# Turning the attention output in 32x32 word blocks on VectorE, with wo read by 8 KB rows

## The chip, the cores and the metric

The kernel runs on one core of a Trainium2 chip. The metric is the device time of one execution in microseconds. On one core there is no second die to compare with, so runs are compared through the kernel before, which ran on the same chip in the same rounds.

## The reference, cut to what matters

Decoding attention with grouped queries: 32 batches, 4 query rows each, 32 query heads on 4 key/value heads, 2048 cached keys, head size 128, all in bf16.

```python
q = (x @ wq).reshape(B, Sq, Hq, Dh)           # B=32, Sq=4, Hq=32, Dh=128
scores = einsum("bhqd,bhkd->bhqk", q, k) * Dh ** -0.5
p = softmax(scores)
o = einsum("bhqk,bhkd->bhqd", p, v)
return o.transpose(0, 2, 1, 3).reshape(B, Sq, Hq * Dh) @ wo
```

K and V are 134 MB, wq and wo 8.4 MB each. Every byte is read once.

## The kernel before: the parts that matter

All reads are issued by SyncE on one DMA queue. Each K or V load is 2 MB, 16 KB per partition. wo follows in 11 pieces after the last V, into buffers that K and V have left. Each piece of more than one head has 4 KB rows:

```python
WO = (4, 4, 4, 4, 4, 4, 2, 2, 2, 1, 1)             # heads per piece of wo
wo_v = wo.rearrange("(h p e) n -> p h (e n)", p=128, e=2)
...
    dst = wo_at(h0, m).rearrange("p (h n) -> p h n", n=2 * D)
    src = wo_v[:, h0 // 2:(h0 + m) // 2, :]        # D = 1024 bf16: rows of 4 KB
```

The output o of each batch comes out of P*V with (group, head, query) on partitions and the head size along the row. The out-projection needs the head size on partitions. Before, TensorE turns each batch with four matmuls against an identity, and ScalarE evicts the result:

```python
def o_evac(i):          # ScalarE: PSUM -> o_sb, scaled by 1/sum
    ...
def pe_ot(i):           # TensorE: four 128x64 matmuls per batch
    ...
            lhsT = o_sb.rearrange("p (d e) -> p e d", e=2)[:, e_, :]
            rhs = ident.rearrange("p (h u s) -> p u h s", u=2, s=Sq)[:, u, :, :]
    ...
def ot_evac(i):         # ScalarE: PSUM -> oT_sb
    ...
```

VectorE transposes every K tile (four 128x1024 word transposes a batch), takes the row maximum and turns the probabilities. TensorE also runs a few idle matmuls per batch.

## Time and profile before

Median 364.49 us of 3 runs (364.45 to 364.68).

| What | Reading before |
|---|---|
| Bytes read from HBM | 151.26 MB |
| DMA rate, 80 to 320 us | 428 GB/s, share 1.01 |
| DMA rate while wo arrives (slices 38 and 39) | 401 and 407 GB/s |
| VectorE busy, 80 to 200 us and 200 to 320 us | 92% and 87% |
| Last wait for wo ends | 358.66 us of a span of 362.4 us |

The DMA engines are full in every slice but the first and the last (90% or more by the page; their share is 1.01 from 10 to 355 us). No compute engine is: the busiest, TensorE, is busy for 85% of the span. The rate dips in slices 38 and 39, to 401 and 407 GB/s from 423 to 434, where wo with its shorter rows arrives.

The groups that the change removes, alters or adds to (the columns are line, engine, operation, tiles, shapes and count, then busy us and mean ns of one, then idle time before and its cause):

```profile
L373 POOL COPY PD_sb<-PT_sb 32x1024 f32<-32x1024 f32 x62 | 64.2, 1036 | 71.1 <-PE ps_r L384 46.3 <-DVE rinv L362 22.0
...
L406 ACT ACTIVATE oT_sb<-ps_r 128x128 bf16<-128x128 f32 x32 | 8.9, 278 | 106.6 <-PE ps_r L401 106.6
L401 PE MATMUL ps_r<-ident,o_sb 128*64 128x64 bf16 x128 | 8.1, 207 | 0.7 <-PEq L85 0.7
...
L362 DVE RECIPROCAL rinv<-ssum 128x1 f32<-128x1 f32 x32 | 3.9, 121 | 0.0
```

### The profile page before, as it was taken

Reading aid. Unit: us, or ns where it says so; the run is one execution under the profiler, and the core shown is the slowest. Engines: PE = TensorE matmul, PEld = TensorE weight load, DVE = VectorE, ACT = ScalarE, POOL = GpSimd, SP = SyncE. Lnnn points to the kernel's source line nnn. Section 1 sums busy time; section 2 is a strip of 40 time slices with the busy share of each in tenths; the row PEclk is TensorE's granted clock in tenths of the full one; section 3 lists DMA queues with packets and bytes.
Section 4 is the critical chain, followed back from the end, with each engine's and each line's share of the span. In section 5 each row is a group of like instructions: output and inputs, shape, how many; then the busy total and the mean of one; then the engine's idle time right before and its main releaser. Section 6 shows DMA issues by size and latency. Waiting matters only on the chain. (4 is left out here: it accounts for less than half of the span.)

```text
span 362.4 us, 6547 instructions
## 1 busy us (share of the span) xinstructions
PE 309.1 (85%) x2991; PEld 142.1 (39%) x2402; DVE 275.8 (76%) x275; ACT 111.4 (31%) x142; POOL 166.1 (46%) x261
## 2 busy tenths in 40 slices
PE   1987777899999999999999998888888889889896
PEld 1002000444444444444444444444333344449711
DVE  0028799999999999999999998898888888856200
ACT  1014222333333333333333333333322233334100
POOL 8002155255555555555555544445555555544000
PEclk9999999999999999999999999999999999999999
DMA  7999999999999999999999999999999999999995
GB/s 324 432 430 434 434 423 423 427 430 430 423 425 427 430 430 424 430 425 430 430 426 427 424 432 432 425 427 427 430 432 425 427 427 431 430 427 427 401 407 195
DMA packets 12589, 151.68 MB, mean 419 GB/s; under 512 B 1312, under 2 KB 1568, under 8 KB 3872
## 3 DMA queue, kind: packets, MB, share of 16 engines
q1 hardware_dynamic: 12432, 151.39, 98.7%
q10 hardware_dynamic: 144, 0.13, 0.1%
q8 instruction: 6, 0.10, 0.1%
q14 instruction: 7, 0.06, 0.0%
HBM read 151.26 MB, written 0.26 MB: 418 GB/s over the span
## 5 line engine op out<-in xcount | busy, mean ns | idle before, releaser
L324 DVE STREAM_TRANSPOSE KT_sb<-big 128x1024 f32<-128x1024 f32 x128 | 150.7, 1217 | 8.9 <-DMA big<-in_k_cache_dram 8.8
L351 ACT ACTIVATE P_sb<-ps_s,negmx 128x2048 bf16<-128x2048 f32 x32 | 82.2, 2568 | 85.3 <-DVE negmx L347 85.3
L16 PE MATMUL ps_s<-KT_sb,QD_sb 128*128 128x512 bf16 x384 | 103.7, 377 | 0.0
L373 POOL COPY PD_sb<-PT_sb 32x1024 f32<-32x1024 f32 x62 | 64.2, 1036 | 71.1 <-PE ps_r L384 46.3
L373 POOL COPY big<-PT_sb 32x1024 f32<-32x1024 f32 x61 | 63.7, 1045 | 59.6 <-PE ps_r L384 28.7
L346 DVE TENSOR_REDUCE mx<-ps_s 128x1 f32<-128x2048 f32 x32 | 73.3, 2292 | 11.0 <-PE ps_s L16 10.0
L384 PE MATMUL ps_r<-big 128*128 128x128 bf16 x1024 | 59.8, 219 | 8.7 <-PEq L85 8.6
L384 PE MATMUL ps_r<-big,PD_sb 128*128 128x128 bf16 x1024 | 59.8, 219 | 7.9 <-PEq L85 7.9
L384 PEld LDWEIGHTS ps_r<-big,PD_sb 128*128 128x128 bf16 x1024 | 58.0, 98 | 19.8 <-issue 18.7
L384 PEld LDWEIGHTS ps_r<-big 128*128 128x128 bf16 x1024 | 58.0, 98 | 19.7 <-issue 18.6
L337 PE MATMUL ps_s<-KT_sb,QD_sb 128*128 128x512 bf16 x128 | 48.3, 377 | 17.3 <-PEq L85 17.3
L337 PEld LDWEIGHTS ps_s<-KT_sb,QD_sb 128*128 128x128 bf16 x128 | 12.3, 96 | 103.1 <-issue 103.1
L361 DVE STREAM_TRANSPOSE PT_sb<-P_sb 128x1024 f32<-128x1024 f32 x32 | 39.9, 1246 | 15.1 <-ACT P_sb L351 15.1
L314 POOL COPY QD_sb<-QT_sb 32x64 f32<-32x64 f32 x128 | 29.6, 231 | 38.1 <-DVE QT_sb L293 20.7
L406 ACT ACTIVATE oT_sb<-ps_r 128x128 bf16<-128x128 f32 x32 | 8.9, 278 | 106.6 <-PE ps_r L401 106.6
L16 PE MATMUL ps_r<-QT_sb,ident 128*128 128x512 bf16 x132 | 33.7, 379 | 4.5 <-issue 4.4
L425 DVE CAST P_sb<-ps_s 128x512 bf16<-128x512 f32 x1 | 0.7, 690 | 22.1 <-PE ps_s L16 22.1
L401 PEld LDWEIGHTS ps_r<-ident,o_sb 128*64 128x64 bf16 x128 | 4.6, 109 | 31.2 <-issue 30.9
L275 DVE CAST KT_sb<-ps_r 128x512 bf16<-128x512 f32 x2 | 1.3, 686 | 20.0 <-PE ps_r L259 20.0
L391 ACT ACTIVATE o_sb<-ps_r,rinv 128x128 bf16<-128x128 f32 x32 | 11.7, 367 | 15.3 <-PE ps_r L384 13.4
L16 PE MATMUL ps_s<-big,oT_sb 128*128 128x512 bf16 x32 | 12.1, 379 | 0.7 <-ACT oT_sb L406 0.7
L416 PE MATMUL ps_s<-big,oT_sb 128*128 128x512 bf16 x30 | 11.4, 380 | 1.1 <-DMA big<-in_wo_dram 1.1
(41 smaller groups left out, 86.1 us busy)
## 6 DMA issues: line engine op xcount, KB each, us to landing
big<-in_k_cache_dram SPq DMA_DIRECT2D x32, 2048.0 KB, 16.9
big<-in_v_cache_dram SPq DMA_DIRECT2D x32, 2048.0 KB, 20.7
big<-in_wq_dram SPq DMA_DIRECT2D x4, 2048.0 KB, 13.9
big<-in_wo_dram SPq DMA_DIRECT2D x6, 1024.0 KB, 21.1
big<-in_wo_dram SPq DMA_DIRECT2D x3, 512.0 KB, 16.0
big<-in_wo_dram SPq DMA_DIRECT2D x2, 256.0 KB, 15.0
P_sb<-in_x_dram SPq DMA_DIRECT2D x1, 256.0 KB, 2.8
out_dram<-P_sb ACTq DMA_DIRECT2D x1, 128.0 KB, 1.8
```

The lines of the kernel that those rows point to most:

```text
L16: return eng.add_instruction(mybir.InstMatmult(name=nc.get_next_instruction_name(), engine=eng.engine, start_tensor_calc=start, stop_tenso ...
L314: p.op("pool", lambda e, s=src, d=dst: e.tensor_copy(d, s), waits if g == 0 else [], ("qd", i) if g == G - 1 else None)
L324: p.op("dve", lambda e, s=src, d=dst: e.transpose(d, s), waits, ("kt", i, c), gives="t_kt" if c == NCH - 1 else None)
L337: mm = lambda e, a_=(out_, lhsT, rhs), f=first, l=last: e.matmul(a_[0], lhsT=a_[1], rhs=a_[2], start=f, stop=l, skip_group_check=True)
L346: p.op("dve", lambda e: e.tensor_reduce(mx[:, i % 4:i % 4 + 1], ps_s[:, :], AX.X, ALU.max), [("qk", i)], ("mx", i))
L351: p.op("act", lambda e: e.activation(P_sb[:, :, :, :].rearrange("p t r w -> p t w r"), ps_s[:, :].rearrange("p (t w r) -> p t w r", w=2, r=R),
L361: p.op("dve", lambda e: e.transpose(dst, src), [("exp", i)] + ([("pd", i - 2, G - 1)] if i > 1 else []), ("pt", i))
L373: p.op("dve" if i >= B - 2 and g < i - B + 4 else "pool", lambda e, s=src, d=dst: e.tensor_copy(d, s), [("pt", i), free], ("pd", i, g))
L384: p.op("pe", lambda e: e.matmul(buf[:, 0:Dh], lhsT=pd_of(i)[:, t // 2, :, :, t % 2].rearrange("p g q -> p (g q)"), rhs=big[:, slot_of("v", ...
L391: p.op("act", lambda e: e.activation(o_sb[:, :], buf[:, 0:Dh], ACT.Copy, scale=rinv[:, i % 4:i % 4 + 1]), [("pv", i), ("rinv", i)] + ([("o ...
L406: p.op("act", lambda e: e.activation(oT_sb[:, :, :, i * Sq:(i + 1) * Sq].rearrange("p h e s -> p e h s"), buf[:, 0:128].rearrange("p (e h ...
L416: mm = lambda e, a=(out_, lhsT, rhs), h=h: e.matmul(a[0], lhsT=a[1], rhs=a[2], start=(h == 0), stop=(h == Hq - 1), skip_group_check=True)
```

## The change

The intent is to take the turning of o from TensorE and ScalarE. VectorE turns o in 32x32 blocks of 4-byte words (two bf16 each), four batches in one instruction (128x128 words), late in the kernel. For that, the rows of P*V are ordered by head mod 4, so that each block of 32 partitions holds one head mod 4. A partition of the turned o then belongs to four neighbouring rows of wo, so wo can be read by rows of 8 KB. The softmax sums still have the old row order, so TensorE permutes them with a one-column fp32 matmul before the reciprocal. The diff, cut to its core:

```diff
-        oT_sb = sbuf("oT_sb", [128, Hq // 2, 2, NT], BF16)
+        oT_sb = sbuf("oT_sb", [128, Hq // 4, 2, B, Sq, 2], BF16)
...
-        wo_v = wo.rearrange("(h p e) n -> p h (e n)", p=128, e=2)
+        wo_v = wo.rearrange("(h p e) n -> p h (e n)", p=128, e=4)
...
+            dst, src = wo_at(u0, m), wo_v[:, u0 // 4, u0 % 4 * D:(u0 % 4 + m) * D]
...
-            p.op("dve", lambda e: e.reciprocal(rinv[...], ssum[...]), [("exp", i)], ("rinv", i))
+        def pe_sum(i):
+            p.op("pe", lambda e: e.matmul(ring[i % 4][:, 511:512], lhsT=permf[:, :], rhs=ssum[:, i % 4:i % 4 + 1], ...))
+        def recip(i):
+            p.op("dve", lambda e: e.reciprocal(rinv[...], ring[i % 4][:, 511:512]), [("ss", i)], ("rinv", i))
...
-        def pe_ot(i): ...        # four matmuls per batch
-        def ot_evac(i): ...      # ScalarE eviction
+        def o_turn(b0, n):
+            for a in range(2):
+                src = words(QT_sb[:, b0:b0 + n, ...])...[:, :, a, :]
+                dst = words(oT_sb[:, :, a, b0:b0 + n, :, :]...)
+                p.op("dve", lambda e, s=src, d=dst: e.transpose(d, s), [("o", b0 + n - 1)], ...)
...
+            if 21 < i and 4 * (i - 22) + 4 <= i - LAG:
+                o_turn(4 * (i - 22), 4)
...
+        for b0, n in ((24, 4), (28, 2), (30, 1), (31, 1)):
+            o_turn(b0, n)
```

The copies that spread the probabilities now write runs of 8 words in place of 32, and the idle matmuls go from 4 of 512 columns to 5 of 384.

More of the change, by code (lines that the diff above doesn't have):

```diff
@@ L135, in bass_standalone__gqa_block_cached__sampling_kernel @@
     WO = (4, 4, 4, 4, 4, 4, 2, 2, 2, 1, 1)
+    IDLE = 384
     scale = float(Dh) ** -0.5
@@ L157, in bass_standalone__gqa_block_cached__sampling_kernel @@
         PT_sb = sbuf("PT_sb", [128, 2, T // 2, 32, 2], BF16)
-        PD_sb = sbuf("PD_sb", [128, T // 2, G, 32, 2], BF16)
-        o_sb = sbuf("o_sb", [128, Dh], BF16)
+        PD_sb = sbuf("PD_sb", [128, T // 2, 4, G, 8, 2], BF16)
         y_sb = P_flat[:, D:2 * D]
@@ L163, in bass_standalone__gqa_block_cached__sampling_kernel @@
         identf = sbuf("identf", [128, 128], F32)
+        permf = sbuf("permf", [128, 128], F32)
         mx = sbuf("mx", [128, 4], F32)
@@ L195, in slot_of @@
             return b % VS if kind == "v" else VS + b % KS
-        PF_sb = big[:, NS - 1, :, :].rearrange("p t d -> p (t d)").rearrange("p (t g q w) -> p t g q w", t=T // 2, g=G, q=32)
+        PF_sb = big[:, NS - 1, :, :].rearrange("p t d -> p (t d)").rearrange("p (t x g q w) -> p t x g q w", t=T // 2, x=4, g=G, q=8)
         for kind, b in loads:
@@ L208, in bass_standalone__gqa_block_cached__sampling_kernel, with wo_at @@
         wo_slot = [slot_of(kind, b) for kind, b in wo_for]
-        def wo_at(h, m):
-            return big[:, wo_slot[h // 8], :, :].rearrange("p t d -> p (t d)")[:, h % 8 * D:(h % 8 + m) * D]
-        wo_v = wo.rearrange("(h p e) n -> p h (e n)", p=128, e=2)
-        h0 = 0
+        def wo_at(u, m):
+            return big[:, wo_slot[u // 8], :, :].rearrange("p t d -> p (t d)")[:, u % 8 * D:(u % 8 + m) * D]
+        wo_v = wo.rearrange("(h p e) n -> p h (e n)", p=128, e=4)
+        u0 = 0
         for c, m in enumerate(WO):
-            assert h0 // 8 == (h0 + m - 1) // 8
-            kind, b = wo_for[h0 // 8]
-            if m > 1:
-                dst = wo_at(h0, m).rearrange("p (h n) -> p h n", n=2 * D)
-                src = wo_v[:, h0 // 2:(h0 + m) // 2, :]
-            else:
-                dst, src = wo_at(h0, 1), wo_v[:, h0 // 2, h0 % 2 * D:(h0 % 2 + 1) * D]
+            assert u0 // 4 == (u0 + m - 1) // 4
+            kind, b = wo_for[u0 // 8]
+            dst, src = wo_at(u0, m), wo_v[:, u0 // 4, u0 % 4 * D:(u0 % 4 + m) * D]
             p.dma("sp", lambda e, dst=dst, src=src: e.dma_start(dst, src),
                 [("kt", b, NCH - 1) if kind == "k" else ("pv", b)], ("wo", c), f"s_wo{c}")
-            h0 += m
-        assert h0 == Hq
+            u0 += m
+        assert u0 == Hq
         p.op("pool", lambda e: e.memset(ident[:], 0.0), [], "ident0")
@@ L233, in bass_standalone__gqa_block_cached__sampling_kernel @@
         p.op("pool", lambda e: e.tensor_copy(identf[:], ident[:]), ["ident"], "identf")
+        p.op("pool", lambda e: e.tensor_copy(
+            permf.rearrange("p (x g r) -> p x g r", x=4, g=G), ident.rearrange("p (g x r) -> p x g r", g=G, x=4)), ["ident"], "permf")
         p.op("pool", lambda e: e.memset(words(QD_sb[:, :, :, :, :, :].rearrange("p i a g q w -> p (i a g q w)")), 0.0), [], "qd0")
-        p.op("pool", lambda e: e.memset(words(PD_sb[:, :, :, :, :].rearrange("p t g q w -> p (t g q w)")), 0.0), [], "pd0")
-        p.op("pool", lambda e: e.memset(words(PF_sb.rearrange("p t g q w -> p (t g q w)")), 0.0), [], "pf0")
+        p.op("pool", lambda e: e.memset(words(PD_sb[:, :, :, :, :, :].rearrange("p t x g q w -> p (t x g q w)")), 0.0), [], "pd0")
+        p.op("pool", lambda e: e.memset(words(PF_sb.rearrange("p t x g q w -> p (t x g q w)")), 0.0), [], "pf0")
         for kt in range(KT):
@@ L270, in bass_standalone__gqa_block_cached__sampling_kernel @@
         for n, j in enumerate(QJ):
-            g, h = j // 2, j % 2 * 4
-            dst = q_sb[:, h:h + 4, :, g, :]
+            g, y = j // 2, j % 2
+            dst = q_sb.rearrange("p (x y) a g e -> p x y a g e", y=2)[:, :, y, :, g, :]
             src = ps_q(j).rearrange("p (h a e) -> p h a e", h=4, a=2)
@@ L354, in softmax_exp @@
                 [("negmx", i)] + ([("pt", i - 1)] if i else ["qproj"]), ("exp", i))
-            if i < L:
-                p.give("act", ("exp", i), "t_exp")
+            p.give("act", ("exp", i), "t_exp")
         def pt(i):
@@ L361, in pt @@
             p.op("dve", lambda e: e.transpose(dst, src), [("exp", i)] + ([("pd", i - 2, G - 1)] if i > 1 else []), ("pt", i))
-            p.op("dve", lambda e: e.reciprocal(rinv[:, i % 4:i % 4 + 1], ssum[:, i % 4:i % 4 + 1]), [("exp", i)], ("rinv", i))
+        def pe_sum(i):
+            p.op("pe", lambda e: e.matmul(ring[i % 4][:, 511:512], lhsT=permf[:, :], rhs=ssum[:, i % 4:i % 4 + 1], start=True, stop=True),
+                 ["permf"] if i == 0 else [], ("ss", i), [("t_exp", 1)] * (i == L))
+        def recip(i):
+            p.op("dve", lambda e: e.reciprocal(rinv[:, i % 4:i % 4 + 1], ring[i % 4][:, 511:512]), [("ss", i)], ("rinv", i))
         def pd_of(i):
@@ L370, in pd @@
                 rows = slice(32 * g, 32 * (g + 1))
-                src = words(PT_sb[rows, i % 2, :, :, :].rearrange("p t q w -> p t (q w)"))
-                dst = words(pd_of(i)[rows, :, g, :, :].rearrange("p t q w -> p t (q w)"))
+                src = words(PT_sb[rows, i % 2, :, :, :].rearrange("p t (x q) w -> p (t x) (q w)", x=4))
+                dst = words(pd_of(i)[rows, :, :, g, :, :].rearrange("p t x q w -> p (t x) (q w)"))
                 p.op("dve" if i >= B - 2 and g < i - B + 4 else "pool", lambda e, s=src, d=dst: e.tensor_copy(d, s), [("pt", i), free], ("pd", i, g))
@@ L384, in pe_pv @@
             p.op("pe", lambda e: e.matmul(
-                buf[:, 0:Dh], lhsT=pd_of(i)[:, t // 2, :, :, t % 2].rearrange("p g q -> p (g q)"),
+                buf[:, 0:Dh], lhsT=pd_of(i)[:, t // 2, :, :, :, t % 2].rearrange("p x g q -> p (x g q)"),
                 rhs=big[:, slot_of("v", i), t, :], start=(t == 0), stop=(t == T - 1)),
@@ L390, in o_evac, with oT_of @@
             buf = ring_of["o", i]
-            p.op("act", lambda e: e.activation(o_sb[:, :], buf[:, 0:Dh], ACT.Copy, scale=rinv[:, i % 4:i % 4 + 1]),
-                 [("pv", i), ("rinv", i)] + ([("oT", i - 1)] if i else []), ("o", i), gives="t_o")
-        def pe_ot(i):
-            buf = ring_of["ot", i] = slot()
-            for e_ in range(2):
-                for u in range(2):
-                    out_ = buf[64 * u:64 * (u + 1), 64 * e_:64 * (e_ + 1)]
-                    lhsT = o_sb.rearrange("p (d e) -> p e d", e=2)[:, e_, :]
-                    rhs = ident.rearrange("p (h u s) -> p u h s", u=2, s=Sq)[:, u, :, :]
-                    p.op("pe", lambda e, a=(out_, lhsT, rhs): e.matmul(a[0], lhsT=a[1], rhs=a[2], start=True, stop=True),
-                         [], ("oT", i) if e_ == u == 1 else None, [("t_o", 1)] if e_ == u == 0 else [])
-        def ot_evac(i):
-            buf = ring_of["ot", i]
-            p.op("act", lambda e: e.activation(
-                oT_sb[:, :, :, i * Sq:(i + 1) * Sq].rearrange("p h e s -> p e h s"),
-                buf[:, 0:128].rearrange("p (e h s) -> p e h s", e=2, s=Sq), ACT.Copy),
-                [("oT", i)], ("ot", i))
+            dst = QT_sb[:, i, :, :, :, :].rearrange("p a h s w -> p (a h s w)").rearrange("p (a d w) -> p a d w", a=2, w=2)
+            src = buf[:, 0:Dh].rearrange("p (d a w) -> p a d w", a=2, w=2)
+            p.op("act", lambda e: e.activation(dst, src, ACT.Copy, scale=rinv[:, i % 4:i % 4 + 1]), [("pv", i), ("rinv", i)], ("o", i))
+        def o_turn(b0, n):
+            for a in range(2):
+                src = words(QT_sb[:, b0:b0 + n, :, :, :, :].rearrange("p b a h s w -> p b (a h s w)")).rearrange(
+                    "p b (a d) -> p b a d", a=2)[:, :, a, :]
+                dst = words(oT_sb[:, :, a, b0:b0 + n, :, :].rearrange("p h b s w -> p h b (s w)")).rearrange("p h b s -> p b h s")
+                p.op("dve", lambda e, s=src, d=dst: e.transpose(d, s), [("o", b0 + n - 1)], ("ot", b0 + n - 1) if a else None)
+        def oT_of(u):
+            return oT_sb[:, u // 4, u % 4 // 2, :, :, u % 2].rearrange("p b s -> p (b s)")
         def oproj(c):
@@ L413, in oproj @@
                 for j in range(2):
-                    out_, lhsT, rhs = ps_s[:, NC * j:NC * (j + 1)], oT_sb[:, h // 2, h % 2, :], wo_at(h, 1)[:, NC * j:NC * (j + 1)]
+                    out_, lhsT, rhs = ps_s[:, NC * j:NC * (j + 1)], oT_of(h), wo_at(h, 1)[:, NC * j:NC * (j + 1)]
                     if j == 0:
@@ L436, in bass_standalone__gqa_block_cached__sampling_kernel @@
         starts = []
+        idle_rhs = ident[:, :].unsqueeze(1).to_broadcast([128, IDLE // 128, 128])
         for i in range(B + LAG):
@@ L445, in bass_standalone__gqa_block_cached__sampling_kernel @@
                 softmax_max(i)
-            if 0 < j < B - LAG:
-                pe_ot(j - 1)
-                ot_evac(j - 1)
+            if 0 < i < B:
+                pe_sum(i - 1)
             if i < B:
-                pe_idle(16 if i < LAG else 4, ring[len(used) % 4], q_flat, [("qb", 3, 1), ("qs", 3)] if i == 0 else [])
+                pe_idle(20 if i < LAG else 5, ring[j % 4][:, 0:IDLE], idle_rhs, [("qb", 3, 1), ("qs", 3)] if i == 0 else [])
                 softmax_exp(i)
+            if 0 < i < B:
+                recip(i - 1)
             if i < L:
                 kt(i + 1, (2, 3))
+            if 21 < i and 4 * (i - 22) + 4 <= i - LAG:
+                o_turn(4 * (i - 22), 4)
             if i < B:
@@ L458, in bass_standalone__gqa_block_cached__sampling_kernel @@
                     pe_pv(j, t)
-                if j >= B - LAG:
-                    pe_ot(j - 1)
-                    ot_evac(j - 1)
+                if i == B:
+                    pe_sum(L)
                 o_evac(j)
+            if i == B:
+                recip(L)
             if 0 < i <= B:
                 pd(i - 1)
-        pe_ot(L)
-        ot_evac(L)
+        for b0, n in ((24, 4), (28, 2), (30, 1), (31, 1)):
+            o_turn(b0, n)
         for c in range(len(WO)):
```

## The prediction

364.49 us measured, less 0.5 us for wo, gives the 364.0 us.

> **What bounds the kernel now.** DMA bandwidth, from about 3 us to 359 us. The page's 40 slices show the DMA engines at 0.99 or 1.0 in every slice but the first and last, moving 423 to 434 GB/s. The kernel must move 151.4 MB.[...] The DMA issue view shows K and V loads (2 MB each, about 4.9 us of transfer) landing 17 and 21 us after issue: three to four loads are always queued, so the queue doesn't run dry. VectorE is busy 93% of 80 to 200 us but only 86% of 220 to 320 us, because it has run ahead of the data. The chain that ended last finishes with wo: last piece landed about 358.7 us, then matmul, eviction (0.69 us) and the output DMA (1.8 us).
>
> **What the change does.**
> - Removed, 32 times each: four TensorE 128x64 matmuls (0.25 us a group), their ScalarE eviction (0.28 us). Idle matmuls go from 4x512 to 5x384 columns, about 0.06 us less by the 0.215 us spacing. None of these lies on the DMA path.
> - Added, 32 times: a one-column fp32 matmul (estimate 0.3 us, from 0.14 us weight load and 0.27 us for the trace's f32 128x128 matmul); the reciprocal now reads PSUM (0.12 us before, perhaps 0.15).
> - Added once: VectorE turns. 128x1024 words take 1.22 us, so 128x128 words should take about 0.2 us: 2.4 us in six iterations in which VectorE has about 1.4 us spare each, and about 1 us at the end.
> - PD/PF copies: runs of 8 words instead of 32 (GpSimd 1.04 us now). If they take 1.0 to 1.5 us, GpSimd goes from about 5.1 to at most 7 us of a 9.8 us period: off the path.
> - wo by 8 KB rows: the only part on the path. The packet records show 614 ns for 16 KB and 161 ns for 4 KB (median), so about 10 ns a packet and 151 ns per 4 KB: an 8 KB packet is estimated at 312 ns. Six pieces (6.3 MB) change from 1536 packets of 4 KB to 768 of 8 KB, over 16 engines: 15.5 us becomes 15.0 us. The last 2 MB keep 4 KB and 2 KB packets.
>
> **On the critical path:** -0.5 us from wo. Everything else falls in slack: the out-projection starts at 343.7 us, needs 64 x 0.215 = 13.8 us, and waits for wo from 350.6 us on; wo pieces wait about 15 us in the queue after issue, so a tail a few microseconds later on VectorE or TensorE costs nothing. Turning the last batches should let the out-projection start about 0.5 us earlier, which only lengthens its waits.
>
> **Predicted:** 364.0 us, range 363.2 to 365.0. Faster by over 2%: 0.01; within 2%: 0.97; slower by over 2%: 0.02.
>
> **What would show each step.** Slices 38 and 39, 401 and 407 GB/s now, rise to about 415 to 422; wo packets of 8 KB take about 312 ns; last wo landing near 358.2 us. DMA share stays 0.99 or more. ScalarE busy falls about 9 us, the four-matmul group and its eviction vanish; GpSimd copies stay below 1.5 us; VectorE turns near 0.2 us, the end still waiting for wo in the chain.
>
> **What would make it wrong.** GpSimd copies doubling or worse with short runs, delaying P*V, V buffers and so loads; the fp32 one-column matmul or its weights costing much more than 0.3 us and holding TensorE; turns with 32-byte strided writes taking several times 0.2 us, delaying the last K buffers and starving wo; 8 KB packets running no faster than 4 KB[...].

## More of the kernel before

The page's first part has the busy time of each engine; of the second part the DMA rows are shown (40 slices of the span, tenths of busy DMA engines, then GB/s); of the third part, the DMA queues with packets, MB and share:

```profile
PE 309.1 (85%) x2991; PEld 142.1 (39%) x2402; DVE 275.8 (76%) x275; ACT 111.4 (31%) x142; POOL 166.1 (46%) x261
...
DMA  7999999999999999999999999999999999999995
GB/s 324 432 430 434 434 423 423 427 430 430 423 425 427 430 430 424 430 425 430 430 426 427 424 432 432 425 427 427 430 432 425 427 427 431 430 427 427 401 407 195
...
q1 hardware_dynamic: 12432, 151.39, 98.7%
q10 hardware_dynamic: 144, 0.13, 0.1%
q8 instruction: 6, 0.10, 0.1%
q14 instruction: 7, 0.06, 0.0%
```

The end of the kernel, first in the chain of waits (start, duration, what), then in the timeline (last P*V and the last wait for wo):

```profile
341.77 15.61 DMA big<-in_wo_dram
357.38 0.04 issue
357.42 0.39 PE ps_s L416
```

```profile
338.38 3.73 PE L384 MATMUL ps_r<-big 128*128 128x128 bf16 x64
...
358.66 0.10 PEld L416 LDWEIGHTS ps_s<-big,oT_sb 128*128 128x128 bf16 x1 [0.48 <-DMA big<-in_wo_dram]
```

The out-projection has to wait for wo to land. From the wait that ends at 357.38 us, eight matmuls, the eviction and the output DMA remain.

## The result

364.56 us median of 6 runs (364.51 to 364.67), against 364.44 us of 6 runs of before (364.27 to 364.68). The ratio is 1.0003, with a 95% interval of 0.999 to 1.0016: the same time. A ratio here is the mean time of one kernel's runs over that of the other's of the same rounds, so it is not quite the ratio of the medians.

The page of the changed kernel, the same lines:

```profile
PE 308.9 (85%) x3002; PEld 147.4 (41%) x2338; DVE 279.1 (77%) x295; ACT 102.7 (28%) x110; POOL 165.9 (46%) x262
...
DMA  8999999999999999999999999999999999999994
GB/s 325 425 432 434 432 430 423 428 423 430 428 423 428 432 426 430 428 427 428 428 427 430 429 426 428 426 430 432 426 428 426 428 431 430 426 428 421 416 416 159
...
q1 hardware_dynamic: 11664, 151.39, 98.4%
q8 instruction: 6, 0.10, 0.1%
q10 hardware_dynamic: 144, 0.13, 0.1%
q14 instruction: 8, 0.07, 0.0%
```

Slices 38 and 39 rose from 401 and 407 to 416 and 416 GB/s, and q1 has 768 packets fewer: wo by longer rows works. Yet the last slice fell from 195 to 159 GB/s: less was moving at the very end. VectorE has 20 more instructions, and the second instruction queue carried 8 packets in place of 7.

The groups that took the place of the removed ones:

```profile
L377 POOL COPY PD_sb<-PT_sb 32x1024 f32<-32x1024 f32 x62 | 64.3, 1036 | 70.1 <-PE ps_r L388 45.2 <-DVE PT_sb L359 22.0
...
L362 PE MATMUL ps_r<-ssum,permf 128*128 128x1 f32 x64 | 8.9, 208 | 0.0
...
L366 DVE RECIPROCAL rinv<-ps_r 128x1 f32<-128x1 f32 x32 | 5.0, 158 | 0.2 <-PE ps_r L362 0.2
...
L404 DVE STREAM_TRANSPOSE oT_sb<-QT_sb 128x128 f32<-128x128 f32 x14 | 3.3, 274 | 0.0
```

The end in the chain of waits, then in the timeline:

```profile
332.70 25.12 DMA big<-in_wo_dram
357.82 0.05 issue
357.87 0.39 PE ps_s L414
```

```profile
339.29 3.73 PE L388 MATMUL ps_r<-big 128*128 128x128 bf16 x64 [1.19 <-PEq L85]
...
359.13 0.10 PEld L414 LDWEIGHTS ps_s<-big,oT_sb 128*128 128x128 bf16 x1 [0.51 <-DMA big<-in_wo_dram]
```

Both ends are about 0.45 us later than before (357.82 against 357.38, and 359.13 against 358.66). The surprise is the other line: P*V of the last batch begins 0.9 us later than before and TensorE idles 1.19 us ahead of it. It needs the last V load. So the delay was there before any of wo was used.

### What the packet records show

The trace also holds every DMA packet, with start, duration, size and queue, but not which of the 16 DMA engines moved it. (From here on, "engine" without a name is a DMA engine.) The records hold 1312 packets of 4 bytes for the 82 transfers of the page, 16 each. So we take it that every load is split over the 16 engines and that each ends its share with such a packet, its mark. By this reading, which fits the time between marks below (eight 16 KB packets of 614 ns are 4.91 us), the mean of these 16 marks tells when the average engine was done, and the end of the last data packet when the slowest was. (The groups of 16 are taken in order of time. An engine that is far behind can exchange a mark with the next load; for the ends, the last data packet is used.) In us of the span:

```
                                        before    after
last V load: mean of 16 engines         336.38   336.55
last V load: slowest engine             337.74   338.65
end of wo:   mean of 16 engines         357.45   357.25
end of wo:   slowest engine             358.16   358.64
slowest, from last V to end of wo        20.42    19.98
```

So the slowest engine needs 0.44 us less for wo, and the mean engine finishes 0.20 us earlier. But the slowest engine came to wo 0.91 us later. The records say when it fell back. In the load just ahead of the last V (mean mark at 331.60 us), the slowest engine went from 1.26 us behind the mean to 2.17 us behind. In that time the records hold an 8 KB packet of the second instruction queue, and right behind it a 16 KB data packet of twice the usual 614 ns:

```
start us   bytes   ns     queue
 332.18     8192    325   q14 (instructions)
 332.50    16384   1273   q1  (V data)
```

If both ran on one engine, the pair cost it 0.325 + 1.273 - 0.614 = 0.98 us, close to the 0.91 us by which the slowest engine fell back. From 50 us on, every 16 KB data packet above 900 ns, 10 in before and 12 after the change, starts within 15 ns of the end of an instruction packet. Before has no instruction packet between 302 and 335 us.

The packet times in the traces of before and after, so far as they matter here:

| Packets | ns each |
|---|---|
| data on q1, 16 KB, 8 KB, 4 KB and 2 KB (medians) | 614, 312, 161 and 84 |
| instructions on q8, 16 KB | 1018 to 1102 |
| instructions on q14, 8 KB, from 50 us on | 309 to 362 |
| 16 KB of data right behind an 8 KB instruction packet, from 50 us on | 960 to 1273 |

The marks support that one engine paid, and show which. Sorted by time, 15 of the 16 marks of that load come 4.89 to 4.90 us after those of the load before it, and the last one 5.86 us after: the engine that was already last lost 0.97 us. They also show why it was last. Before holds two pairs of the same form (a fetch of 325 ns, then a data packet of 1273 ns), at 80.62 and 206.46 us, when 61 and 187 of VectorE's recorded instructions had started. Each made a single mark later by 0.97 us: one went from 0.09 to 1.06 us after the fourth-earliest mark of its load, and later one from 1.09 to 2.06 us, which made it the last. In the changed kernel the three pairs come at VectorE's 62nd, 187th and 312th. So these look like VectorE's own fetches, all on one engine, which is the slowest because of them.

The ends follow the slowest engine. The waits end about 0.5 us after the last data packet (358.66 against 358.16, and 359.13 against 358.64).

### The profile page after: what moved, and what is told of

It is laid out like the page before. It is cut to its first block, busy times and chain, and to the rows that moved or that the text cites. A ratio compares the mean times of both kernels' runs of the same rounds, so it can differ in the third digit from the quotient of the medians.

```text
span 362.8 us, 6454 instructions
## 1 busy us (share of the span) xinstructions
PE 308.9 (85%) x3002; PEld 147.4 (41%) x2338; DVE 279.1 (77%) x295; ACT 102.7 (28%) x110; POOL 165.9 (46%) x262
## 2 busy tenths in 40 slices
DMA packets 11822, 151.69 MB, mean 418 GB/s; under 512 B 1312, under 2 KB 1568, under 8 KB 2336
## 5 line engine op out<-in xcount | busy, mean ns | idle before, releaser
L16 PE MATMUL ps_s<-KT_sb,QD_sb 128*128 128x512 bf16 x384 | 105.0, 381 | 0.0
L377 POOL COPY PD_sb<-PT_sb 32x1024 f32<-32x1024 f32 x62 | 64.3, 1036 | 70.1 <-PE ps_r L388 45.2
L377 POOL COPY big<-PT_sb 32x1024 f32<-32x1024 f32 x61 | 63.2, 1036 | 60.4 <-PE ps_r L388 35.9
L336 PE MATMUL ps_s<-KT_sb,QD_sb 128*128 128x512 bf16 x128 | 48.7, 381 | 21.9 <-PEq L85 21.9
L16 PE MATMUL ps_r<-ident 128*128 128x384 bf16 x173 | 33.3, 325 | 0.0
L362 PEld LDWEIGHTS ps_r<-ssum,permf 128*128 128x128 f32 x64 | 11.9, 187 | 24.8 <-issue 23.1
L397 ACT ACTIVATE QT_sb<-ps_r,rinv 128x128 bf16<-128x128 f32 x32 | 11.8, 368 | 24.1 <-PE ps_r L388 21.6
L414 PE MATMUL ps_s<-big,oT_sb 128*128 128x512 bf16 x32 | 12.2, 380 | 2.2 <-DMA big<-in_wo_dram 1.2
L16 PE MATMUL ps_s<-big,oT_sb 128*128 128x512 bf16 x32 | 12.1, 379 | 0.0
L247 PE MATMUL ps_r<-ident 128*128 128x384 bf16 x32 | 10.3, 323 | 0.0
```

The source lines that it names most:

```text
L16: return eng.add_instruction(mybir.InstMatmult(name=nc.get_next_instruction_name(), engine=eng.engine, start_tensor_calc=start, stop_tenso ...
L336: mm = lambda e, a_=(out_, lhsT, rhs), f=first, l=last: e.matmul(a_[0], lhsT=a_[1], rhs=a_[2], start=f, stop=l, skip_group_check=True)
L362: p.op("pe", lambda e: e.matmul(ring[i % 4][:, 511:512], lhsT=permf[:, :], rhs=ssum[:, i % 4:i % 4 + 1], start=True, stop=True), ["permf"] ...
L377: p.op("dve" if i >= B - 2 and g < i - B + 4 else "pool", lambda e, s=src, d=dst: e.tensor_copy(d, s), [("pt", i), free], ("pd", i, g))
L397: p.op("act", lambda e: e.activation(dst, src, ACT.Copy, scale=rinv[:, i % 4:i % 4 + 1]), [("pv", i), ("rinv", i)], ("o", i))
L414: mm = lambda e, a=(out_, lhsT, rhs), h=h: e.matmul(a[0], lhsT=a[1], rhs=a[2], start=(h == 0), stop=(h == Hq - 1), skip_group_check=True)
```

## The theories

- **Theory A.** The 20 turns made VectorE's instruction stream longer by enough to need one more 8 KB piece. Its fetch runs on a DMA engine that is already the slowest, and makes it 0.9 us later. All engines are full while wo arrives (share 1.00 from 335 to 355 us in the changed kernel), so, by this theory, the slowest doesn't make up for it, and its lateness reaches the end of the kernel. It eats the 0.44 us that the longer rows save.
- **Rival B.** The longer rows of wo save nothing at the end, or lengthening VectorE's stream costs nothing: something else ends last.
- **Rival C.** The turns cost VectorE's time, or its order, and that delays loads.
- **Rival D.** Small added instructions late in the kernel disturb the loads by themselves, on whatever engine.

In the expectations below, times of fetches were read with the packets' clock set 0.5 us later than here; "332.7 us" there is the fetch at 332.18 us. A "page" there stands for the 8192 bytes of one q14 packet; that the length of the stream, or reaching a "page boundary", brings the next one is the theory that the runs test.

## The experiments

Each was run in 5 rounds beside before.

### The changed kernel again

No edit.

> The changed kernel itself, as the base for the three runs beside it on the same chip. All theories: 364.4 to 364.7 us, ratio to before 1.000 to 1.001, an 8 KB instruction fetch at about 332.7 us of the span, the slowest of the 16 DMA engines finishing the last V load about 2.1 us after the mean engine, while the others' last is 1.3 us after it.

364.80 us median (364.49 to 364.93), before 364.42, ratio 1.0007. Fetch at 332.52 us, slowest engine 2.47 us behind at the last V. The numbers repeat, with the slowest engine a little further behind.

### Turns merged from 20 instructions to 4

```diff
-            for a in range(2):
-                src = ...[:, :, a, :]           # one half, 32 words per batch
+            src = words(QT_sb[:, b0:b0 + n, ...])            # both halves
+            dst = words(oT_sb[:, :, :, b0:b0 + n, :, :]...).rearrange("p h a b s -> p b a h s")
...
-            if 21 < i and 4 * (i - 22) + 4 <= i - LAG:
-                o_turn(4 * (i - 22), 4)
+            if i == 27:
+                o_turn(0, 24)
...
-        for b0, n in ((24, 4), (28, 2), (30, 1), (31, 1)):
+        for b0, n in ((24, 6), (30, 1), (31, 1)):
```

> The changed kernel with its 20 VectorE turns merged into 4, so that VectorE's stream is 16 instructions shorter; the same words are turned. Theory A (the turns lengthened VectorE's instruction stream past one more 8 KB page; its fetch at 332.7 us runs on the DMA engine that is already last and makes it 0.9 us later, which eats the 0.45 us that wo's longer rows save): the fetch disappears or moves to after the last wo packet, the slowest engine is back at about 1.3 us behind the mean, and the time falls by 0.6 to 0.9 us to 363.7 to 364.0 us, 0.5 us below before. Rival B (wo's longer rows save nothing at the end because something else ends last, TensorE or the final pieces): unchanged, 364.4 to 364.7. Rival C (the loss is VectorE's time for the turns): they still cost about 3 us in all, so at most 0.2 us better.

363.74 us median (363.58 to 363.82), before 364.42, ratio 0.9981 (0.9967 to 0.9994). That is 1.06 us less than the changed kernel. The result is correct. The queue line and the start of the last P*V of this run:

```profile
q14 instruction: 7, 0.06, 0.0%
```

```profile
338.48 3.73 PE L388 MATMUL ps_r<-big 128*128 128x128 bf16 x64 [0.50 <-PEq L85]
...
343.04 0.38 PE L412 MATMUL ps_s<-big,oT_sb 128*128 128x512 bf16 x1 [0.83 <-DVE oT_sb L402]
```

The fetch near 332 us is gone (one at 335.87 us stays, which the changed kernel has too, at 335.92), the last P*V starts within 0.1 us of where it did before (338.48 against 338.38), and the out-projection starts 0.9 us earlier than in before or after. The slowest engine is 1.33 us behind at the last V, as before. Rival B expected no change. Rival C, whose bound was 0.2 us, doesn't fit 1.06 us. But the turns take 2.8 us here and 4.2 us in the changed kernel, so this run alone doesn't exclude it; the runs with late memsets below do.

### wo by 4 KB runs in the changed kernel

Two pieces of wo that lie in one buffer exchange halves, so that each reads two runs of 4 KB per partition. DMAs, bytes and instructions stay the same in number.

```diff
+            if m == 4:
+                r = c % 2 * 2 * D
+                dst = big[:, wo_slot[u0 // 8], :, :]....rearrange("p (h n) -> p h n", h=2)[:, :, r:r + 2 * D]
+                src = wo_v[:, c // 2 * 2:c // 2 * 2 + 2, r:r + 2 * D]
...
+            if WO[c] == 4:
+                hs = [c // 2 * 8 + c % 2 * 2 + k for k in (0, 1, 4, 5)]
```

> The changed kernel with its first six wo pieces read as two 4 KB runs a partition in place of one 8 KB run; the same number of DMAs, bytes and instructions per piece. Theory A: wo's packets return from 312 to 161 ns for half the bytes, every engine needs 0.43 to 0.5 us more for wo, and the time rises to 364.9 to 365.1 us. Rival B: wo's rows don't show at the end, 364.4 to 364.7 us.

365.28 us median (364.99 to 365.37), ratio 1.0021 to before. It is 0.48 us over the changed kernel beside it. The absolute time missed the expected 364.9 to 365.1 because the base was 364.80, not 364.56. The packets are back at 161 ns for 4 KB, and the slowest engine takes 20.40 us for wo in place of 19.98.

### Both edits

> Both edits: 4 merged turns and 4 KB rows. Theory A: the two effects add, so about 0.45 us over the run with merged turns alone, 364.1 to 364.5 us, near before. Rival B: equal to the changed kernel. If the effects don't add (difference under 0.2 us), the theory of one slowest engine that sets the end is wrong.

364.29 us median (364.00 to 364.35), ratio 0.9994. The four runs form a square, medians in us:

| | with the extra fetch (20 turns) | without (4 turns) | difference |
|---|---|---|---|
| wo by 8 KB rows | 364.80 | 363.74 | 1.06 |
| wo by 4 KB runs | 365.28 | 364.29 | 0.99 |
| difference | 0.48 | 0.55 | |

The effects add. The rows are worth about 0.5 us on the critical path, as predicted, and whatever came with the 20 turns costs about 1.0 us.

### The kernel before with 20 VectorE memsets where the turns are

```diff
+            if 21 < i <= 27:
+                pad(2, "dve")       # memsets of one scratch column each
...
+        pad(8, "dve")               # ahead of the last turn of o
```

> The kernel before with 20 one-column VectorE memsets of a scratch tile, placed where the change puts its 20 turns (two in each of six late iterations, eight at the end). Nothing else changes. Theory A: VectorE's stream crosses the same page boundary, an 8 KB instruction fetch appears at about 332 us of the span, the slowest DMA engine falls about 0.9 us further behind, and the time rises by 0.6 to 0.95 us to 365.0 to 365.4 us. Rival B: VectorE has slack,[...] 364.3 to 364.6 us.

365.13 us median (365.01 to 365.52), before 364.36, ratio 1.0025 (1.0011 to 1.0039). The extra 8 KB fetch is there, but at 337.93 us, not near 332. It fell in the wo phase: the slowest engine was 1.40 us behind at the last V and 1.55 us behind at the end of wo, where before it is 0.72 us behind. The cost of 0.77 us is as expected; the time of the fetch was missed. Its pair is cheaper here: the fetch took 326 ns and the 4 KB packet of wo behind it 496 ns in place of 161, so 0.66 us in all where a 16 KB packet of V made it 0.98.

### The same memsets after VectorE's last copy

```diff
         oproj_out()
+        pad(20)
```

> The same 20 memsets, all placed after VectorE's last copy, when the last wo packet has landed. The stream is as long as in the run with pads in the loop. Theory A: the page boundary is reached only after the last data packet, so any fetch comes too late to delay a load; 364.3 to 364.7 us. If the program's length itself costs (for example at the start), 0.5 us or more slower.

365.07 us median (364.86 to 365.43), ratio 1.002. This expectation failed, and it is the most telling run. The queue line and VectorE's timeline at the end:

```profile
q14 instruction: 8, 0.07, 0.0%
```

```profile
360.28 0.69 DVE L433 CAST P_sb<-ps_s 128x512 bf16<-128x512 f32 x1 [23.05 <-PE ps_s L16]
360.92 0.31 DVE L306 MEMSET scr<- 128x1 f32 x20
```

The memsets run at 360.92 us, after the last data packet at 359.12 us, so their execution cannot have delayed a load. But the fetch came at 338.37 us, while VectorE sat waiting for its last copy. The kernel is 0.71 us slower for instructions that had not run yet. That separates the length of the stream from the work in it: Rival C has no place here.

### The same memsets on GpSimd

> The same 20 memsets in the same places, on GpSimd. Its stream has some 365 recorded instructions and fetches near the 70th, 198th and 325th, so 20 to 40 more reach no new page. Theory A: no new fetch, 364.3 to 364.6 us. Rival D (added small instructions in the late iterations disturb the loads by themselves): slower by 0.3 us or more, as with VectorE.

The edit is the one with pads in the loop, with the engine exchanged. 364.48 us median (364.29 to 364.66), ratio 1.0003. No new fetch:

```profile
q14 instruction: 7, 0.06, 0.0%
```

Rival D falls: the same small instructions in the same places cost 0.12 us by the medians, which is within the spread, where they brought no fetch.

### 148 VectorE memsets

Seven in each of twenty iterations and eight at the end.

> The kernel before with 148 VectorE memsets (seven in each of twenty iterations, eight at the end): one page more than the run with 20. Theory A: two fetches more than before on the same DMA engine, the slowest engine falls 1.2 to 1.9 us further behind than in before and the time rises by about as much, to 365.6 to 366.3 us, provided that VectorE still keeps ahead of the loads ([...]0.8 to 1.4 us spare). Rival B: no change.

366.03 us median (365.80 to 366.09), before 364.36, ratio 1.0044 (1.0030 to 1.0058). It is 1.67 us slower, with two packets more than before:

```profile
q14 instruction: 9, 0.07, 0.0%
```

The slowest engine is already 2.32 us behind at the last V (before 1.36) and then takes a fetch in the wo phase too. The pairs of VectorE's form show it: 80.63, 161.81 and 234.37 us in place of 80.62 and 206.46, and a fetch at 339.06 us. The two added pairs cost 0.98 and 0.67 us, 1.65 us together. In both the runs of before with 20 and with 148 memsets it takes about 21.36 us for wo in place of 20.42.

### Merged turns once more, and with their stream made long again

> The changed kernel with 4 merged turns once more, as the base for the run beside it and to see whether its gain repeats on another chip or call. Theory A: 363.6 to 363.9 us, no 8 KB fetch at 332 to 334 us, ratio to before 0.997 to 0.999.

363.69 us median (363.61 to 363.84), before 364.38, ratio 0.9979 (0.9966 to 0.9993). The gain repeats on another chip.

The edit adds 16 memsets after VectorE's last copy to the merged turns:

```diff
         oproj_out()
+        pad(16)
```

> The 4 merged turns with 16 VectorE memsets after VectorE's last copy, which makes its stream as long again as the changed kernel's (built again with a scratch tile of 16 columns, since the first build ran out of SBUF). The memsets run after the last wo packet, so their work can't delay a load. Theory A: the fetch returns (at 338 to 340 us, as in the run of before with late pads), and the time rises by 0.6 to 1.0 us over the merged turns alone, to 364.3 to 364.8 us, ratio to before 0.999 to 1.001. Rival C (the merged turns gained by taking less of VectorE's time, or by other order): stays at 363.6 to 363.9 us, ratio 0.998.

364.74 us median of 6 runs (364.56 to 364.81), before 364.38, ratio 1.0001. One run of before took 1804 us; the ratio doesn't use it. Another took 366.52 us and one 365.02 us, and these pull the ratio, which is of means, down to 1.0001, while the medians differ by 0.36 us.

```profile
q14 instruction: 8, 0.07, 0.0%
```

The gain of the merged turns is gone, with the same merged turns in the same places. (The two runs of merged turns are from different chips; before took 364.38 us in both.) The fetch came at 335.29 us (earlier than expected), with the slowest engine 2.32 us behind at the last V. Merging gained by making the stream shorter, not by taking less of VectorE's time.

### All runs in one table

"Behind" is the end of the last data packet minus the mean of the last 16 marks. VectorE's instructions are those that the trace records, waits included.

| Run | VectorE instructions | q14 packets | slowest behind at end, us | slowest engine's wo time, us | median us |
|---|---|---|---|---|---|
| before | 310 | 7 | 0.72 | 20.42 | 364.36 to 364.49 |
| before, GpSimd memsets | 310 | 7 | 0.79 | 20.42 | 364.48 |
| merged turns | 313 | 7 | 0.76, 0.59 | 20.00, 20.01 | 363.74, 363.69 |
| merged turns, 4 KB runs | 313 | 7 | 0.84 | 20.42 | 364.29 |
| changed kernel | 329 | 8 | 1.38, 1.62 | 19.98, 19.98 | 364.56, 364.80 |
| changed kernel, 4 KB runs | 329 | 8 | 1.63 | 20.40 | 365.28 |
| merged turns, late memsets | 329 | 8 | 1.47 | 19.99 | 364.74 |
| before, 20 memsets | 330 | 8 | 1.55 | 21.37 | 365.13 |
| before, 20 late memsets | 330 | 8 | 1.39 | 21.37 | 365.07 |
| before, 148 memsets | 458 | 9 | 2.25 | 21.35 | 366.03 |

The number of packets sorts the runs without an exception: 0.6 to 0.8 us behind with seven, 1.4 to 1.6 with eight, 2.25 with nine.

## Why the prediction was right and where it failed

The number held: 364.56 us lies in the range of 363.2 to 365.0, and "within 2%" was right. That says little, since the range also holds the time of the kernel before; with a gain and a cost that nearly cancelled, it was partly luck. The sign of the step inside it did not hold: the text forecast -0.5 us, and the difference of the medians is +0.12 us.

- **"On the critical path: -0.5 us from wo."** Right in mechanism and size. 8 KB packets take 312 ns as estimated. 768 of them in place of 1536 of 161 ns, over 16 engines, is 0.48 us; the square of runs gives 0.48 and 0.55 us.
- **"Everything else falls in slack."** This is the step that failed. It costed every added instruction by its duration and left out that instructions also arrive by DMA (6 packets on q8 and 8 on q14 in the changed kernel), on engines whose share was already 1.01. VectorE's stream went from 310 to 329 recorded instructions, and with a length somewhere between 313 and 329 came one more 8 KB fetch (seven packets on q14 at 313, eight at 329). Its price is 0.7 us where it fell after the last V (pads in before) and 1.0 us in the changed kernel. The sum should have read -0.5 + 1.0 = +0.5 us at most; measured were +0.12 us and +0.38 us, by medians. In the square, the run with both edits, which has neither the long rows nor the extra fetch, is 0.13 us below before, within the spread; -0.13 - 0.55 + 1.06 is the +0.38 of the second call. The first call's +0.12 is 0.26 us less, inside the 0.44 us spread of the second call's runs.
- **"The queue doesn't run dry."** Right (share 1.01 from 10 to 355 us in both kernels), and the cost was not hidden. In the changed kernel the slowest engine came to wo 0.91 us later than in before, took 0.44 us less for it and ended 0.48 us later, so it made up nothing of what the fetch had cost. The mean engine ended wo 0.20 us earlier than in before, and the time followed the slowest.
- **"A tail a few microseconds later on VectorE or TensorE costs nothing."** Consistent with the runs: P*V of the last batch started 0.9 us later in the changed kernel, and TensorE still waited for wo afterwards.
- **"Slices 38 and 39 rise to about 415 to 422."** Right: 416 and 416. (The text's first lines, 423 to 434 GB/s in every slice but the first and last, had overlooked these two.) **"Last wo landing near 358.2 us"**: wrong, the last wait ended at 359.13 us. With the fetch taken out it would have been met: 358.32 us with merged turns, by this line of its timeline:

```profile
358.32 0.10 PEld L412 LDWEIGHTS ps_s<-big,oT_sb 128*128 128x128 bf16 x1 [0.46 <-DMA big<-in_wo_dram]
```

- **"The out-projection starts about 0.5 us earlier."** Not in the changed kernel, at 343.92 against 343.94 us, since the last V came late. With merged turns it started at 343.04.
- **Durations.** A 128x128 word turn took 274 ns where 0.2 us was estimated; the one-column matmul is two instructions of 208 ns that overlap, 8.9 us busy for 32 pairs or 0.28 us each, near the 0.3 us estimated; the reciprocal, which now reads PSUM, took 158 ns where 0.15 us was guessed, against 121 ns from SBUF before; ScalarE's busy time fell by 8.7 us of the 9 expected; GpSimd's copies with runs of 8 words took 1036 ns as before, so that fear was empty. The granted clock was 0.995 in four of the six runs and 1.0 in two, and these two were the slowest and the fastest.

The version with merged turns beats both kernels, by about 0.7 us on before (ratios 0.9981 and 0.9979, both intervals below 1). It is well under 2%, and the runs' spreads don't overlap: 363.58 to 363.84 in ten runs, against no run of before below 364.12.

**What stays open.** Which instruction triggers the fetch is not settled: it came about when the 312th recorded VectorE instruction had started in the changed kernel, at the 307th with late memsets, and at the 327th with the 20 memsets in the loop. That the extra packet belongs to VectorE follows from the experiments (memsets on VectorE bring it, on GpSimd not) and from its form and place among VectorE's instructions, not from a label. That it fell on the slowest engine is shown by the marks where it came ahead of the last V; in the wo phase it is inferred from that engine's lateness, since the records don't name engines. In all runs with 4 KB rows, before included, another fetch comes at 345 to 347 us, and in all with 8 KB rows at 335.6 to 336.3 us; what moves it is unknown, and the table shows no effect of it.

## What to carry to other kernels

In this kernel, where the share of the DMA engines is 1.01 from 10 to 355 us, the time followed the slowest engine, and what else travelled on that one cost time: one more 8 KB packet of instructions cost 0.7 to 1.1 us. It even slowed work that comes earlier in the program: with memsets that ran at 360.92 us the fetch came at 338.37 us. Not every fetch did: the one at 335.6 to 336.3 us shows no effect in the table. Before trusting that an added instruction "falls in slack", count instructions per engine as well as their durations, and compare the instruction lines of the DMA queues. The time that instructions take is not their whole price: 20 late memsets took 0.31 us of VectorE's time, after the last load, and cost 0.71 us, and 20 turns merged into 4 gained 1.06 us.
